# Rows of 320 columns instead of 384: the last transposition takes columns 192 to 320, and the low parts go to the lower half of the partitions

## Chip, core and metric

The kernel runs on one core of a Trainium2 chip. The metric is the device time of one execution in microseconds (us), as the median of several runs. TensorE is called PE, VectorE DVE, ScalarE ACT, GpSimd POOL and SyncE SP, as in the profile.

## The reference

Three stages run one after the other: a gated linear attention over 768 steps for 2 x 8 heads of 40 columns, a mixture of 8 experts of which each of the 1536 rows takes two, and a feed-forward layer with the activation h·cos(h). A row has 320 columns throughout.

```python
for t in range(S):                       # attention, S = 768
    m_new = np.maximum(f_gate[:, :, t] + m, i_gate[:, :, t])
    ...
    h_tilde = np.einsum('bhde,bhe->bhd', C, qt)
    denom = np.maximum(np.abs(nq), 1.0)
    y[:, :, t] = o * h_tilde / denom

for e in range(E):                       # experts, E = 8, 320 -> 1024 -> 320
    for k in range(2):
        mask = top2[:, k] == e
        h = np.maximum(x[mask] @ w1[e], 0.0)
        out[mask] += top2_w[mask, k, None] * (h @ w2[e])

h = x @ w_in                             # 320 -> 2048 -> 320
g = h * np.cos(h)
return (g @ w_out).astype(np.float32)
```

## The kernel before

**Split numbers.** The matrix products must come out in float32 precision. Each operand is split into a high part, rounded to the format that PE multiplies fast, and a low part, the rest. `mm1` (L585) forms a product of rows and first weights out of eight matmuls: high times high, high times low and low times high for two blocks of 128 columns, and two for the last block.

**The last block.** 320 columns are two blocks of 128 and one of 64. In the last one the partitions 0 to 63 hold the high parts of columns 256 to 319 and the partitions 64 to 127 the low parts of the same columns; the weights lie there twice (`pack`, L1118). One matmul over 128 partitions then gives high times weight plus low times weight. For this, every row is 384 columns long (`KW`) before the change: its last 64 columns are a copy of columns 256 to 319, and transposing columns 256 to 383 puts the same numbers in both halves. `prep_x` (L547) transposes three blocks of up to 128 rows into PSUM, ACT copies them rounded into `xh` (L553), DVE writes the low parts of the first two blocks (L554) and the low parts of partitions 64 to 127 of the third in place (L555).

**Where rows are made.** In the attention a chunk n of 128 rows ends in `mk_y` (L315): DVE writes 320 columns of the tile `xt` (L327), POOL copies the last 64 (L329), SP stores the rows in `XD` in DRAM (L330). PE transposes the same tile for the router (`rt_a`, L337). The experts' rows are fetched from `XD` by indirect DMAs that POOL issues (`gather`, L537). After the experts `comb` (L669) adds the two results of a row on DVE (L674), a second DVE instruction copies the last 64 columns (L675), and `comb_t` hands the tile to `prep_x`.

**Order.** Each engine works through its own queue in order. The order is written out by hand: `att_step` (L850) for the twelve chunks, and a table of steps (`put`, L905) for the rest. In POOL's queue the copy of chunk n stands between the state decay of the next chunk (L277) and two triangular masks (`mk_w`, L210); behind these come a weight split (`split`, L573, L582) and, in chunk 9, the first two gathers. In SP's queue the store of chunk n (L330) stands ahead of weight loads (L528). In the last phase `comb` runs beside the conversion of the last layer's weights (`conv_ops`, L697) and the layer's own steps (`moe2_step`, L787).

Of the kernel before, what the change touches and what calls it, by code (L numbers as in the profile page):

```python
# [9 lines left out]
FT = mybir.dt.float32  # L10
# [10 lines left out]
C = 128  # L21
# [19 lines left out]
def tile_mlstm_moe_moe2(ctx, tc, qk, kv, og, gi, gf, wcat, noise, wm1, wm2, cst, out):  # L41
# [105 lines left out]
    XD = dr.tile([B * S, KW], FT, name="xd")  # L147
# [167 lines left out]
    def mk_y(n):  # L315
# [10 lines left out]
        x = d["x"] = mp.tile([128, KW], FT, name="xt", bufs=3)  # L326
        V.scalar_tensor_tensor(out=x[:, :DM].rearrange("p (h e) -> p h e", e=D), in0=pv[:, :, 0:D], scalar=0.5,  # L327
                               in1=o, op0=OP.mult, op1=OP.mult)
        G.tensor_copy(x[:, DM:KW], x[:, 256:DM])  # L329
# [6 lines left out]

    def rt_a(n, ps_=None):  # L337
        b, c = divmod(n, NC)
        d = L[n]
        p = (ps_ or psM)()  # L340
        for k in range(3):
            T.transpose(p[:, 128 * k:128 * k + 128], d["x"][:, 128 * k:128 * k + 128], ident)
        d["xT"] = ap_.tile([128, 3, 128], FT, name="xTt", bufs=2)
        A.activation(d["xT"], p[:, :KW].rearrange("p (k t) -> p k t", t=128), AF.Copy)
# [192 lines left out]
    def gather(g, i):  # L537
# [3 lines left out]
        t = mp.tile([128, KW], FT, name="xgt", tag="xg", bufs=6)  # L541
# [5 lines left out]
    def prep_x(src, np_, xh, xl, n0, ps_=None):  # L547
        p = (ps_ or psM)()
        pv = p[:, :3 * np_].rearrange("p (k t) -> p k t", t=np_)
        for k in range(3):  # L550
            T.transpose(pv[:, k, :], src[:np_, 128 * k:128 * k + 128], ident[:np_, :np_])  # L551
# [3 lines left out]
        V.tensor_tensor(out=xh[64:128, 2, sl], in0=pv[64:128, 2, :], in1=xh[64:128, 2, sl].bitcast(FT),  # L555
# [53 lines left out]
    def fin1(g):  # L609
        d = GX[g]  # L610
        for i, n in enumerate(groups[g][1]):
            t = (mp.tile([128, KW], FT, name="xt", bufs=3) if i == 3 else
# [56 lines left out]
    def comb(b, c):  # L669
# [3 lines left out]
        x = mp.tile([128, KW], FT, name="xt", bufs=3)  # L673
        V.scalar_tensor_tensor(out=x[:, :DM], in0=y1, scalar=r["w"][:, 1, c:c + 1], in1=y0, op0=OP.mult, op1=OP.add)  # L674
        V.tensor_copy(x[:, DM:KW], x[:, 256:DM])  # L675
# [354 lines left out]
    with tc.If(over > 0):  # L1030
# [9 lines left out]
        for b in range(B):  # L1040
            with tc.For_i(0, NC, 1) as it:
                x = mp.tile([128, KW], FT, name="xt", bufs=3)
# [4 lines left out]
                for k in range(3):  # L1047
                    T.transpose(p[:, 128 * k:128 * k + 128], x[:, 128 * k:128 * k + 128], ident)
                xT = wp.tile([128, 384], FT, name="m_t", tag="ct", bufs=3)
                A.activation(xT, p[:, :KW], AF.Copy)  # L1050
                x2 = mp.tile([128, KW], FT, name="xt", bufs=3)
                V.memset(x2, 0.0)
                for e in range(E):
                    acc = psA()
                    for f in range(8):
# [3 lines left out]
                        for k in range(3):  # L1059
                            n = 64 if k == 2 else 128  # L1060
                            T.matmul(p[:, :C], w[:n, 128 * k:128 * k + 128], xT[:n, 128 * k:128 * k + 128],
# [6 lines left out]
                V.tensor_copy(x2[:, DM:KW], x2[:, 256:DM])  # L1068
# [21 lines left out]
def layout(inp):  # L1090
# [23 lines left out]
    w[0] = wg[0:128]; w[1] = wg[128:256]; w[2, :64] = wg[256:]  # L1114
# [44 lines left out]
```

## Time and profile before

| | |
|---|---|
| median of 3 runs | 524.96 us (522.64 to 525.19) |
| the profiled execution | 525.03 us, of which the trace spans 523.3 us |
| PE busy | 490.2 us (94% of the span) |
| DVE busy | 372.1 us (71%) |
| ACT busy | 325.7 us (62%) |
| POOL busy | 278.5 us (53%) |
| chain that ended last | PE 69%, DVE 14%, DMA 7% |

The attention ends at about 110 us, the experts run from 94 to 334 us and the last layer from 334 to 516 us, with overlaps. A time at the start of a row counts from the start of the span. A gap ahead of an instruction stands in brackets behind it, with what ended it.

### The profile page before, as it was taken

The page shows a single profiled execution, that of the slowest core. Times are in us where ns is not written, and L with a number is a line of the kernel's source. Part 1 is how long each engine was busy: PE and PEld are TensorE (multiplying, and loading weights), DVE is VectorE, ACT ScalarE, POOL GpSimd, SP SyncE. Part 2 cuts the span into 40 slices and gives each one's busy share as a digit, 9 for nine tenths or more (in the row PEclk, how much of TensorE's full clock was granted, in tenths as well). Part 3 has the DMA queues.
Part 4 walks back from the last instruction along what each step waited for, and adds up shares of the span by engine and source line. Part 5 has one row for each costly group of instructions (what it writes and reads, how often), then busy time and mean ns, then how long its engine had stood idle before and what let it go on. Part 6 is the DMA issues. An engine that isn't in the chain of part 4 may idle for free.

```text
span 523.3 us, 9036 instructions
## 1 busy us (share of the span) xinstructions
PE 490.2 (94%) x3198; PEld 468.1 (89%) x3198; DVE 372.1 (71%) x791; ACT 325.7 (62%) x695; POOL 278.5 (53%) x246
## 2 busy tenths in 40 slices
PE   4799998999999999999999987999999999999994
PEld 3688887999899999999999976899999999999994
DVE  8774497678378777777775689688856665787772
ACT  3647867466465454545454655578787777777772
POOL 6445468665846867685857696274365347300000
PEclk9999999899999999999999999999999999999998
DMA  6789894695563828291929193030021003001001
GB/s 182 209 281 266 279 278 155 188 363 172 216 248 117 313 88 330 69 372 44 380 88 319 42 360 105 29 115 14 0 76 39 1 8 95 13 2 39 1 1 44
DMA packets 25909, 77.69 MB, mean 148 GB/s; under 512 B 3872, under 2 KB 11552, under 8 KB 25856
## 3 DMA queue, kind: packets, MB, share of 16 engines
q1 hardware_dynamic: 22752, 67.50, 37.2%
q0 software_dynamic: 3104, 9.54, 6.1%
q8 instruction: 27, 0.44, 0.3%
q14 instruction: 26, 0.21, 0.1%
HBM read 67.41 MB, written 9.62 MB: 147 GB/s over the span
## 4 chain that ended last, share of the span: by engine, by line
PE 69%; DVE 14%; DMA 7%; issue 4%; ACT 3%; POOL 2%; SPq 0%; DVEq 0%; POOLq 0%; ACTq 0%
PE pS L589 31%; PE pA L598 9%; PE pA L595 9%; PE pA L594 9%; DMA gb<-gd 2%; DMA xgt<-xd,idx 2%; PE pM L551 2%; PE pS L310 2%; PE pA L247 1%; PE pM L351 1%; PE pA L607 1%; PE pA L606 1%; POOL wl L582 1%; DVE xt L674 1%; DVE c_t L713 1%
## 5 line engine op out<-in xcount | busy, mean ns | idle before, releaser
L582 POOL TENSOR_TENSOR wl<-wraw,wh 128x704 fp32r<-128x704 f32 x69 | 122.9, 1787 | 59.9 <-ACT wh L580 56.3
L644 DVE SCALAR_TENSOR_TENSOR hb<-pS,hb 128x384 fp32r<-128x384 f32 (+2 forms) x128 | 45.9, 390 | 46.4 <-ACT hb L641 45.8
L580 ACT ACTIVATE wh<-wraw 128x704 fp32r<-128x704 f32 x80 | 62.8, 785 | 14.6 <-PE pA L606 8.2
L589 PE MATMUL pS<-xh,wh 128*128 128x448 f32 (+1 forms) x240 | 69.5, 344 | 0.4 <-ACT xh L553 0.4
L589 PE MATMUL pS<-xh,wl 128*128 128x448 f32 (+1 forms) x240 | 66.3, 330 | 0.9 <-POOL wl L582 0.9
L589 PE MATMUL pS<-xh,w 128*128 128x384 f32 x288 | 66.4, 339 | 0.5 <-DVE m_t L754 0.5
L594 PE MATMUL pA<-wh,hb 128*128 128x320 f32 x208 | 62.2, 309 | 0.0
L595 PE MATMUL pA<-wl,hb 128*128 128x320 f32 x208 | 62.2, 309 | 0.0
L739 ACT ACTIVATE m_t<-pS,magic 128x384 f32<-128x384 f32 x64 | 37.1, 579 | 30.4 <-PE pS L589 29.3
L641 ACT ACTIVATE hb<-pS 128x448 fp32r<-128x448 f32 (+1 forms) x80 | 37.6, 471 | 26.9 <-PE pS L589 20.0
L589 PEld LDWEIGHTS pS<-xh,w 128*128 128x128 f32 x288 | 50.0, 188 | 1.2 <-DVE m_t L754 1.1
L598 PE MATMUL pA<-wh,hb 128*128 128x320 f32 x208 | 44.3, 313 | 4.0 <-DVE hb L644 4.0
L754 DVE SCALAR_TENSOR_TENSOR m_t<-m_t,pS 128x384 f32<-128x384 f32 x64 | 35.4, 553 | 15.4 <-ACT m_t L753 15.1
L589 PEld LDWEIGHTS pS<-xh,wl 128*128 128x128 f32 x240 | 43.1, 190 | 3.3 <-POOL wl L582 1.1
L740 DVE TENSOR_SCALAR m_t<-m_t 128x384 f32<-128x384 f32 x64 | 23.3, 365 | 28.8 <-ACT m_t L739 28.6
L589 PEld LDWEIGHTS pS<-xh,wh 128*128 128x128 f32 x240 | 40.9, 190 | 1.4 <-ACT xh L553 0.6
L760 POOL TENSOR_TENSOR wl<-m_t,wh 128x384 fp32r<-128x384 f32 x25 | 25.4, 1017 | 31.0 <-ACT wh L758 21.7
L589 PE MATMUL pS<-xl,wh 128*128 128x448 f32 (+1 forms) x160 | 39.6, 329 | 0.0
L594 PEld LDWEIGHTS pA<-wh,hb 128*128 128x128 f32 x208 | 38.6, 186 | 0.6
L595 PEld LDWEIGHTS pA<-wl,hb 128*128 128x128 f32 x208 | 38.7, 186 | 0.6
L598 PEld LDWEIGHTS pA<-wh,hb 128*128 128x128 f32 x208 | 33.0, 186 | 6.0 <-DVE hb L644 5.9
L542 POOL DMA_INDIRECT xgt<-xd,idx x28 | 34.0, 1215 | 7.8 <-issue 3.4
(203 smaller groups left out, 1251.0 us busy)
## 6 DMA issues: line engine op xcount, KB each, us to landing
wraw<-wm SPq DMA_DIRECT2D x36, 704.0 KB
raw<-wm SPq DMA_DIRECT2D x16, 704.0 KB
qk<-qk SPq DMA_DIRECT2D x24, 240.0 KB
gb<-gd SPq DMA_DIRECT2D x10, 512.0 KB
kv<-kv SPq DMA_DIRECT2D x12, 324.0 KB
yd<-yt SPq DMA_DIRECT2D x22, 160.0 KB
wraw<-wm SPq DMA_DIRECT2D x8, 352.0 KB
xd<-xt SPq DMA_DIRECT2D x12, 192.0 KB
```

Of the source, the lines that this page charges most:

```text
L542: G.indirect_dma_start(out=t[:n, :], out_offset=None, in_=XD[0:S, :] if g < 2 else XD[:, :], in_offset=bass.IndirectOffsetOnAxis(ap=(idxe ...
L580: A.activation(wh, raw[:, f, :], AF.Copy)
L582: eng.tensor_tensor(out=wl, in0=raw[:, f, :], in1=wh.bitcast(FT), op=OP.subtract)
L589: T.matmul(p[:, :n], w[:, 128 * k:128 * k + 128], x[:, m, :], start=(i == 0), stop=(i == 7))
L594: T.matmul(a[:n, :DM], hh[:, s], wh[:, KW:], start=first, stop=False)
L595: T.matmul(a[:n, :DM], hh[:, s], wl[:, KW:], start=False, stop=False)
L598: T.matmul(a[:n, :DM], hl[:, s], wh[:, KW:], start=False, stop=last)
L641: A.activation(hh[:, :n], p[:, :n], AF.Relu)
L644: V.scalar_tensor_tensor(out=hb[:, o:o + z - a], in0=p[:, a:z], scalar=0.0, in1=hh[:, a:z].bitcast(FT), op0=OP.max, op1=OP.subtract)
L739: A.activation(t, m["p"], AF.Identity, bias=magic, scale=0.5 / PI)
L754: V.scalar_tensor_tensor(out=s, in0=s, scalar=1.0, in1=m["p"], op0=OP.subtract, op1=OP.mult)
L760: eng.tensor_tensor(out=m["hl"], in0=m["t"], in1=m["hh"].bitcast(FT), op=OP.subtract)
```

## The change

The rows of `xt`, `xg` and `XD` become 320 columns long. The two copies are gone. The third transposition takes columns 192 to 319: its partitions 64 to 127 get columns 256 to 319, and its partitions 0 to 63 get columns 192 to 255, which the second block has already. ACT copies all three blocks as before. DVE then writes the low parts, which it works out from partitions 64 to 127, to partitions 0 to 63. In the router the last block's weights move to partitions 64 to 127 and the others are zero. A path that runs only when an expert gets too many rows is changed alike and does not run here.

```diff
-    XD = dr.tile([B * S, KW], FT, name="xd")
+    XD = dr.tile([B * S, DM], FT, name="xd")
...
-        x = d["x"] = mp.tile([128, KW], FT, name="xt", bufs=3)
-        V.scalar_tensor_tensor(out=x[:, :DM].rearrange("p (h e) -> p h e", e=D), in0=pv[:, :, 0:D], scalar=0.5,
+        x = d["x"] = mp.tile([128, DM], FT, name="xt", bufs=3)
+        V.scalar_tensor_tensor(out=x.rearrange("p (h e) -> p h e", e=D), in0=pv[:, :, 0:D], scalar=0.5,
                                in1=o, op0=OP.mult, op1=OP.mult)
-        G.tensor_copy(x[:, DM:KW], x[:, 256:DM])
         Y.dma_start(XD[b * S + c * C:b * S + (c + 1) * C, :], x)
...
+    def cols(x, n, k):
+
+        c0 = min(128 * k, DM - 128)
+        return x[:n, c0:c0 + 128]
...
-            T.transpose(p[:, 128 * k:128 * k + 128], d["x"][:, 128 * k:128 * k + 128], ident)
+            T.transpose(p[:, 128 * k:128 * k + 128], cols(d["x"], 128, k), ident)
...
-        t = mp.tile([128, KW], FT, name="xgt", tag="xg", bufs=6)
+        t = mp.tile([128, DM], FT, name="xgt", tag="xg", bufs=6)
...
-            T.transpose(pv[:, k, :], src[:np_, 128 * k:128 * k + 128], ident[:np_, :np_])
+            T.transpose(pv[:, k, :], cols(src, np_, k), ident[:np_, :np_])
         sl = slice(n0, n0 + np_)
         A.activation(xh[:, :, sl], pv, AF.Copy)
         V.tensor_tensor(out=xl[:, :, sl], in0=pv[:, 0:2, :], in1=xh[:, 0:2, sl].bitcast(FT), op=OP.subtract)
-        V.tensor_tensor(out=xh[64:128, 2, sl], in0=pv[64:128, 2, :], in1=xh[64:128, 2, sl].bitcast(FT),
+
+        V.tensor_tensor(out=xh[0:64, 2, sl], in0=pv[64:128, 2, :], in1=xh[64:128, 2, sl].bitcast(FT),
                         op=OP.subtract)
...
-        x = mp.tile([128, KW], FT, name="xt", bufs=3)
-        V.scalar_tensor_tensor(out=x[:, :DM], in0=y1, scalar=r["w"][:, 1, c:c + 1], in1=y0, op0=OP.mult, op1=OP.add)
-        V.tensor_copy(x[:, DM:KW], x[:, 256:DM])
+        x = mp.tile([128, DM], FT, name="xt", bufs=3)
+        V.scalar_tensor_tensor(out=x, in0=y1, scalar=r["w"][:, 1, c:c + 1], in1=y0, op0=OP.mult, op1=OP.add)
...
-    w[0] = wg[0:128]; w[1] = wg[128:256]; w[2, :64] = wg[256:]
+    w[0] = wg[0:128]; w[1] = wg[128:256]; w[2, 64:] = wg[256:]
```

What moves is seen on three queues. POOL's queue at chunks 8 and 9, where the masks (L210) are followed by the first weight split (L582, after the change L587) and the first gathers (L542, after it L546):

```order
-L329 COPY xt<-xt 128x64 [waits DMAHW0_49,DVE_49,Pool_49]
-L210 AFFINE_SELECT wt<-wt 128x512 [waits Activation_49] x2
-L582 TENSOR_TENSOR wl<-wraw,wh 128x704 [waits DMAHW6_49,Activation_49]
+L210 AFFINE_SELECT wt<-wt 128x512 [waits Activation_49,Pool_49]
+L210 AFFINE_SELECT wt<-wt 128x512 [waits Activation_49]
+L587 TENSOR_TENSOR wl<-wraw,wh 128x704 [waits DMAHW6_49,Activation_49]
 L229 TENSOR_TENSOR kb_95<-kv,kdec 128x8x40 [waits DMAHW2_49]
 L277 TENSOR_TENSOR st_99<-st_101,get 40x4x41 [waits DVE_49,PE_49,Activation_49]
 L277 TENSOR_TENSOR st_99<-st_101,get 40x4x41 [waits DVE_49,Activation_49,Pool_49]
-L542 DMA xgt<-xd,idxe 128x384 [waits DVE_49,Pool_49]
-L542 DMA xgt<-xd,idxe 112x384
-L329 COPY xt<-xt 128x64 [waits DMAHW5_49,DVE_49]
+L546 DMA xgt<-xd,idxe 128x320 [waits DMAHW0_49,DMAHW3_49,DVE_49,Pool_49]
+L546 DMA xgt<-xd,idxe 112x320
```

The masks no longer stand behind an instruction that waits for DVE; the first gather now names the stores of its rows itself, which the copies had waited for on its behalf.

SP's queue at chunk 9, the store of the rows and three weight loads behind it, first before and then after:

```order
L330 DMA xd<-xt 128x384 [waits DMAHW2_49,Pool_49]
L528 DMA wraw<-wm 128x704 [waits DMAHW3_49]
L528 DMA wraw<-wm 128x704 [waits DMAHW4_49]
L528 DMA wraw<-wm 128x704 [waits DMAHW5_49]
```

```order
L329 DMA xd<-xt 128x320 [waits DMAHW2_49,DVE_49]
L532 DMA wraw<-wm 128x704 [waits DMAHW3_49]
L532 DMA wraw<-wm 128x704 [waits DMAHW4_49]
L532 DMA wraw<-wm 128x704 [waits DMAHW5_49]
```

The store waits for DVE instead of POOL; the order is the same.

DVE's queue at the first two results of `comb` (L674, after the change L679), with a step of the weight conversion behind each (`w2q` and `c_t`), first before and then after:

```order
L674 SCALAR_TENSOR_TENSOR xt<-yg,r_w_1075 128x320 [waits DMASW1_49,Activation_49]
L675 COPY xt<-xt 128x64 [waits DVE_49]
L723 TENSOR_TENSOR w2q<-c_t_3676,w2q 128x704 [waits DMAHW3_49,DMAHW2_49,Activation_49]
L644 SCALAR_TENSOR_TENSOR hb<-pS,hb 128x240 [waits Activation_49]
L619 COPY yt<-pA 112x320 [waits DMAHW1_49,PE_49]
L674 SCALAR_TENSOR_TENSOR xt<-yg,r_w_1075 128x320 [waits DMAHW2_49,DMASW3_49,Activation_49]
L675 COPY xt<-xt 128x64 [waits DVE_49]
L713 SCALAR_TENSOR_TENSOR c_t_3725<-raw_3583,c_t_3725 128x704
```

```order
L679 SCALAR_TENSOR_TENSOR xt<-yg,r_w_1065 128x320 [waits DMASW1_49,Activation_49]
L727 TENSOR_TENSOR w2q<-c_t_3664,w2q 128x704 [waits DMAHW3_49,DMAHW2_49,Activation_49]
L649 SCALAR_TENSOR_TENSOR hb<-pS,hb 128x240 [waits Activation_49]
L624 COPY yt<-pA 112x320 [waits DMAHW1_49,PE_49]
L679 SCALAR_TENSOR_TENSOR xt<-yg,r_w_1065 128x320 [waits DMAHW2_49,DMASW3_49,Activation_49]
L717 SCALAR_TENSOR_TENSOR c_t_3713<-raw_3571,c_t_3713 128x704 [waits DVE_49]
```

The copies drop out, and the instruction behind the second one carries the wait for DVE that the copy had carried. PE's and ACT's queues keep their instructions and their order.

## Rows read from the trace of the kernel before

**Rows 1.** Busy time by stretch: stretch, length, engines, TensorE clock, DMA share, GB/s

```profile
75.00:92.00 17.00, 14.16 (x120) 12.44 (x118) 13.05 (x28) 10.96 (x31) 14.39 (x19) 1.00 0.60 192
92.00:96.00 4.00, 3.65 (x19) 3.65 (x20) 2.90 (x8) 1.69 (x4) 3.00 (x3) 0.57 0.89 266
133.00:300.00 167.00, 166.52 (x1006) 159.69 (x1005) 118.83 (x204) 87.69 (x154) 116.67 (x72) 1.00 0.55 204
300.00:340.00 40.00, 33.77 (x243) 31.47 (x241) 32.48 (x51) 22.22 (x45) 24.20 (x17) 1.00 0.46 166
355.00:375.00 20.00, 19.16 (x121) 18.57 (x120) 18.04 (x35) 15.95 (x34) 6.35 (x7) 1.00 0.01 4
375.00:515.00 140.00, 139.86 (x874) 138.26 (x873) 95.23 (x203) 106.93 (x222) 41.05 (x41) 1.00 0.09 26
```

**Rows 2.** Groups by line and shape: busy us, mean ns, idle before it

```profile
L555 DVE TENSOR_TENSOR xh<-pM,xh 64x128 fp32r<-64x128 f32 x30 | 8.8, 295 | 0.4
...
L675 DVE COPY xt<-xt 128x64 f32<-128x64 f32 x12 | 3.7, 312 | 0.4
L329 POOL COPY xt<-xt 128x64 f32<-128x64 f32 x12 | 3.7, 307 | 26.0 <-DVE xt L327 17.7 <-issue 8.3
```

**Rows 3.** POOL's timeline, chunks 8 and 9: start, us, instruction, gap before

```profile
81.44 0.84 POOL L329 COPY xt<-xt 128x64 f32<-128x64 f32 x1 [1.50 <-issue]
...
87.80 1.23 POOL L542 DMA_INDIRECT xgt<-xd,idxe  x1 [0.61 <-DVE den L323]
...
90.32 0.23 POOL L329 COPY xt<-xt 128x64 f32<-128x64 f32 x1
```

**Rows 4.** PE's timeline: the waits for POOL and for gathers

```profile
85.83 0.96 PE L266 MATMUL pS<-kv,kb 128*104 128x82 f32 x8 [1.05 <-POOL kb L229]
...
92.35 0.82 PE L551 MATMUL pA<-ident,xgt 112*128 112x112 f32 x3 [0.62 <-DMA xgt<-xd,idxe]
...
176.44 0.52 PE L551 MATMUL pM<-ident,xgt 128*128 128x128 f32 x3 [0.48 <-DMA xgt<-xd,idx]
```

**Rows 5.** DVE's timeline, chunk 9: the gather's indices and the rows' end

```profile
86.68 0.17 DVE L511 TENSOR_SCALAR idxe<-idx 128x4 uint32<-128x4 f32 x1
...
88.01 0.49 DVE L327 SCALAR_TENSOR_TENSOR xt<-pS,ogt 128x320 f32<-128x320 f32 x1
```

**Rows 6.** SP's timeline, chunk 9: the three weight loads behind the store

```profile
90.96 1.46 SPq L528 DMA_DIRECT2D wraw<-wm  x3
```

**Rows 7.** Landing of the gathers issued at 89.33 and at 100.42, us

```profile
DMA to landing us min/median/max: 3.0/3.0/3.0
...
DMA to landing us min/median/max: 5.6/5.6/5.6
```

**Rows 8.** DVE's timeline, last phase: copies and what stands around them

```profile
317.38 1.59 DVE L675 COPY xt<-xt 128x64 f32<-128x64 f32 x1
...
321.70 0.20 DVE L675 COPY xt<-xt 128x64 f32<-128x64 f32 x1
...
328.93 1.93 DVE L723 TENSOR_TENSOR w2q<-c_t,w2q 128x704 fp32r<-128x704 f32 x1
...
369.01 0.42 DVE L554 TENSOR_TENSOR xl<-pM,xh 128x256 fp32r<-128x256 f32 x1 [0.15 <-ACT xh L553]
```

**Rows 9.** POOL's timeline, the weight splits beside the first copy and beside L723

```profile
317.02 1.89 POOL L582 TENSOR_TENSOR wl<-wraw,wh 128x704 fp32r<-128x704 f32 x1
...
328.39 1.72 POOL L582 TENSOR_TENSOR wl<-wraw,wh 128x704 fp32r<-128x704 f32 x1 [3.92 <-ACT wh L580]
```

**Rows 10.** PE's timeline, last phase: its waits for DVE

```profile
325.54 0.56 PE L598 MATMUL pA<-wh,hb 128*128 128x320 f32 x2 [0.44 <-DVE hb L644]
...
372.00 0.96 PE L589 MATMUL pS<-xh,w2q 128*128 128x384 f32 x4 [0.83 <-DVE m_t L754]
```

**Rows 11.** DVE's timeline, start: same shape, without and with another partition block

```profile
9.73 0.28 DVE L109 TENSOR_TENSOR g_all<-g_all 16x128 f32<-16x128 f32 x1
10.04 0.28 DVE L110 TENSOR_TENSOR g_all<-g_all 16x128 f32<-16x128 f32 x1
```

More of the change, by code (lines that the diff above doesn't have):

```diff
@@ L611, in fin1 @@
         for i, n in enumerate(groups[g][1]):
-            t = (mp.tile([128, KW], FT, name="xt", bufs=3) if i == 3 else
+            t = (mp.tile([128, DM], FT, name="xt", bufs=3) if i == 3 else
                  mp.tile([128, DM], FT, name="yt", tag="yt", bufs=3))
@@ L1041, in tile_mlstm_moe_moe2 @@
             with tc.For_i(0, NC, 1) as it:
-                x = mp.tile([128, KW], FT, name="xt", bufs=3)
+                x = mp.tile([128, DM], FT, name="xt", bufs=3)
                 Y.dma_start(x, XD[bass.ds(it * C + b * S, C), :])
@@ L1047, in tile_mlstm_moe_moe2 @@
                 for k in range(3):
-                    T.transpose(p[:, 128 * k:128 * k + 128], x[:, 128 * k:128 * k + 128], ident)
+                    T.transpose(p[:, 128 * k:128 * k + 128], cols(x, 128, k), ident)
                 xT = wp.tile([128, 384], FT, name="m_t", tag="ct", bufs=3)
                 A.activation(xT, p[:, :KW], AF.Copy)
-                x2 = mp.tile([128, KW], FT, name="xt", bufs=3)
+                x2 = mp.tile([128, DM], FT, name="xt", bufs=3)
                 V.memset(x2, 0.0)
@@ L1059, in tile_mlstm_moe_moe2 @@
                         for k in range(3):
-                            n = 64 if k == 2 else 128
-                            T.matmul(p[:, :C], w[:n, 128 * k:128 * k + 128], xT[:n, 128 * k:128 * k + 128],
+                            r = slice(64 * (k == 2), 128)
+                            T.matmul(p[:, :C], w[r, 128 * k:128 * k + 128], xT[r, 128 * k:128 * k + 128],
                                      start=(k == 0), stop=(k == 2))
@@ L1067, in tile_mlstm_moe_moe2 @@
                                            in1=x2[:, :DM], op0=OP.mult, op1=OP.add)
-                V.tensor_copy(x2[:, DM:KW], x2[:, 256:DM])
                 d = {}
```

## Prediction

> **What bounds the kernel now.** I read the page's shares first, then the busy time by stretch, then the waits and timelines of the stretches in which PE idles. PE is full for 166.52 of the 167 us of the experts' main part and for 139.86 of the 140 us after 375 us [rows 1]. In these stretches a saving on another engine, or in a DMA that already comes in time, is worth nothing, and no matmul or transposition is removed. The change can gain only where PE idles and something that it removes or moves ends the wait: 75 to 92 us (17.00 less 14.16 is 2.84 us idle), 300 to 340 us (6.23 us idle, DVE busy 32.48 of 40) and 355 to 375 us (0.84 us idle, DVE busy 18.04 of 20) [rows 1]. Together that is some 10 us, of which most belongs to waits that the copies do not cause. One gather of the main part adds a wait of 0.48 us [rows 4].
>
> **What is removed, as busy time.** Twelve copies on POOL, 3.7 us, and twelve on DVE, 3.7 us [rows 2]. Each row of XD loses 256 bytes: 12 stores of 32 KB less and 32 gathers of up to 32 KB less. That is not yet time; each place is taken by itself.
>
> **The copies on POOL.** They stand in POOL's queue behind a wait for DVE: 17.7 of the 26.0 us of idle time ahead of them was ended by L327 [rows 2]. Up to 75 us I cost this at nothing: PE is busy with the attention's matmuls there and none of its waits was for the copy. At chunk 8 POOL is late. It idles 1.50 us, then the copy takes 0.84 us, 81.44 to 82.28 [rows 3], and the masks, the first weight split and `kb` come behind it; PE waits 1.05 us for `kb` at 85.83 [rows 4]. Without the copy the masks start earlier. But PE then only reaches its next wait sooner: the second transposition of gathered rows, at 92.35, waits for its gather [rows 4], and that chain sets the time. The first gather was issued at 87.80 [rows 3], while its indices were ready at 86.68 + 0.17 = 86.85 [rows 5]. So an earlier POOL can pull the gathers forward by at most 87.80 - 86.85 = 0.95 us. The least is nothing, if what held POOL until 87.80 was DVE, as the wait's label says. I take 0.4 us, about the middle.
>
> **The stores.** At chunk 9 the store of the rows waited for the copy that POOL ran behind both gathers, until 90.32 + 0.23 = 90.55 [rows 3]; now it waits for DVE, which ended at 88.01 + 0.49 = 88.50 [rows 5]. Queued behind it on SP are three weight loads, issued from 90.96 [rows 6]. They leave 2.05 us earlier, and so can meet the gathers. I cost that at nothing in the forecast, since a transfer issued at 88.9 would move most of its data after the gathers, as the heavy traffic of 92 to 96 us (266 GB/s) followed the loads of 90.96 [rows 1, 6]; the other case is a rival. At the other chunks an earlier store gains nothing, as PE waits for no load there.
>
> **Shorter rows.** The one wait of the main part for a gather is 0.48 us at 176.44 [rows 4]. A row that is a sixth shorter takes something off it, between 0 and the whole 0.48; I take 0.2 us, because other loads share that transfer. The other gathers of that stretch land in time.
>
> **The copies on DVE.** Of the twelve, the six after 375 us lie beside a full PE [rows 1]: nothing. Three stand between 317 and 325 us. The first lasts 1.59 us against 0.20 us for the second [rows 8], and that looks like the prize. It started at 317.38, while POOL ran a weight split from 317.02 to 318.91 [rows 9], and it ended at 318.97, just behind it. So it was held. What comes next without it is L723, and an L723 at 328.93, beside another split of POOL that ended at 330.11, lasted 1.93 us and ended 0.75 us behind it [rows 8, 9]. So L723 will be held by the same split, and the gain is only what the copy did after the split, some 0.06 us. I take 0.1 us. The Trainium skill says the same more generally (SBUF — State Buffer, "SBUF: two separate sides"): GpSimd and VectorE instructions in a two-port mode or with two SBUF inputs take a shared port pair as an exclusive lock, and the loser waits for the whole instruction. It speaks against this change, and the trace agrees (1.59 us against 0.20). Read without the lock, the first copy would give 1.59 us instead of 0.1.
>
> The second and third copy are free of that: 0.20 us each [rows 8]. PE waits for DVE 0.44 us at 325.54 [rows 10]; of the 0.4 us I take half to reach it, since the additions between them are also held by splits. So this stretch gives 0.1 + 0.2 = 0.3 us, with bounds 0 and 0.5.
>
> The last three copies stand between 355 and 375 us, where DVE is 90% busy. Two of them are followed by a DVE instruction that waits for ACT (0.15 us at 369.01 [rows 8]), that is, for a transposition by a PE that was not late: the gain is spent in that wait. The third is followed by no such wait, and PE waits 0.83 us for DVE at 372.00 [rows 10]: 0.2 us, with bounds 0 and 0.6 (all three).
>
> **The moved low parts.** L555 now reads partitions 64 to 127 and writes 0 to 63. It lasts 295 ns [rows 2] and runs 44 times. The nearest row of DVE that writes another block of partitions than it reads is L110 (0 to 15, to 32 to 47): 0.28 us, as its neighbour L109 of the same shape without a shift [rows 11]. So I cost it at nothing. L555 is no busier, no longer and waits for the same ACT copy. The transpositions read other columns of the same tile at the same size: nothing.
>
> **The sum.** 0.4 + 0.2 + 0.3 + 0.2 = 1.1 us off the profiled execution's own 525.03 us gives 523.9. That execution lies 0.07 us above the median of 524.96, so I leave it there. From the bounds alone the gain is between 0 and 0.95 + 0.48 + 0.5 + 0.6 = 2.5 us: 522.5 to 525.0.
>
> **Rivals.**
>
> *The clock's dip goes.* Between 92 and 96 us the granted clock is 0.57, between the levels of 1.2 and 2.4 GHz, after PE had idled 2.84 of 17 us [rows 1]. The dip costs 4.00 x (1 - 0.57) = 1.7 us. If `kb` comes in time and the gathers earlier, PE idles less ahead of it and the dip may shrink or go. For it speaks that 1.05 of the 2.84 us was the wait for `kb` [rows 4]; against it, that this wait is likely to reappear as a longer one for the gather. Time: 523.9 - 1.7 = 522.2.
>
> *The weight loads meet the gathers (slower).* Place: chunk 9. The three loads now leave at about 88.9, beside gathers issued between 87.4 and 89. A gather at 89.33 without such company landed after 3.0 us, one at 100.42 behind other transfers after 5.6 us [rows 7]. If the second gather takes the latter, PE's wait at 92.35 grows by 5.6 - 3.0 = 2.6 us: 523.9 + 2.6 = 526.5. It decides from the point at which the loads' data begin to flow before the second gather's are through. For it speaks that SP is free then; against it, the delay between issue and heavy traffic seen above. By the Trainium skill (DMA: Bandwidth & Descriptors, "Queues, rings and completion order") a DMA engine takes turns between its queues packet by packet, which would make this cheaper; the landing of 5.6 us says that company costs, whatever the turns.
>
> *Nothing arrives.* The earlier POOL only meets DVE's short instructions elsewhere and holds them, the gather stays bound to DVE, and the 0.2 us pieces sink in other waits. Time: 525.0.
>
> **Chances.** Forecast 0.55, dip gone 0.17, loads meet gathers 0.14, nothing arrives 0.10, something that I have not seen 0.04. A measurement of this kernel can tell 0.5%, that is 2.6 us, from no change: faster means below 522.3, slower above 527.6. Faster takes most of the dip's 0.17 and the edge of the forecast: 0.21. Slower takes the far end of the collision and half of the unseen: 0.06. The rest, 0.73, is no change that can be told. The range reaches from just below the dip's time, 522.0, to just below the collision's, 526.3.
>
> **What would show it.** Right: POOL's masks at chunk 8 start before 81 us and PE's wait at 85.83 shrinks; the first gather is issued within 0.6 us of its indices; L723 beside POOL's split near 317 us lasts over 1.5 us in the copy's place; L555 stays at 295 ns; PE stays full from 133 to 300 and after 375 us. Wrong: L555 takes longer; the gathers of chunk 9 land after more than 4 us; the clock stays full between 92 and 96 us; or the stretch from 300 to 340 us loses more than 0.5 us, which would mean that the lock is not what held the first copy.

## The result, and the profile after

| | before | after | ratio, 95% interval |
|---|---|---|---|
| first comparison, median of 5 and 5 runs | 524.37 us | 528.19 us | 1.0083 [1.0057, 1.0109] |
| a second comparison, of 24 and 7 runs | 523.58 us | 526.69 us | 1.0059 [1.0036, 1.0082] |
| the profiled execution of after | | 526.06 us, span 524.0 us | |

The change makes the kernel some 3 to 4 us slower. Of that, some 0.4 us lie outside the span of the traces: the time is longer than the span by 1.65 to 1.83 us in every run of the kernel before that has its span on record, and by 2.06 to 2.24 us in every run of after. No run says what these 0.4 us are. The forecast was 523.9 us, with a range of 522.0 to 526.3. The trace shown here is that of the fastest of the first five executions; a second trace of the same kernel, with a span of 525.9 us, is told of below.

The busy time by stretch, after; it answers to [rows 1] and has its columns:

```profile
75.00:92.00 17.00, 14.71 (x105) 13.27 (x105) 12.00 (x27) 10.24 (x29) 11.32 (x13) 0.84 0.53 177
92.00:96.00 4.00, 1.74 (x9) 1.45 (x8) 0.82 (x3) 0.94 (x2) 1.55 (x2) 0.50 0.34 136
133.00:300.00 167.00, 166.53 (x1007) 159.43 (x1006) 120.65 (x208) 87.93 (x154) 116.94 (x73) 1.00 0.54 199
300.00:340.00 40.00, 36.58 (x257) 34.99 (x257) 31.95 (x49) 23.34 (x46) 27.52 (x18) 0.96 0.47 168
355.00:375.00 20.00, 19.44 (x122) 19.02 (x122) 17.19 (x33) 16.59 (x34) 7.64 (x8) 1.00 0.03 9
375.00:515.00 140.00, 140.00 (x878) 138.93 (x877) 95.36 (x199) 107.83 (x224) 41.16 (x41) 1.00 0.09 26
```

Between 92 and 96 us PE is busy for 1.74 us of 4 where it was for 3.65, and the clock is at its lower level, 1.2 GHz (0.50). From 300 us on PE idles less than before. So the loss lies in one place, around 90 us. PE's timeline there, after, against [rows 4]:

```profile
83.73 0.93 PE L266 MATMUL pS<-kv,kb 128*104 128x82 f32 x8 [0.35 <-issue]
85.70 0.42 PE L306 MATMUL pS<-st,qtt 128*128 128x82 f32 x2 [1.03 <-DVE r_hi L513]
91.39 0.90 PE L555 MATMUL pA<-ident,xgt 128*128 128x128 f32 x3 [0.49 <-DMA xgt<-xd,idxe]
94.56 0.82 PE L555 MATMUL pA<-ident,xgt 112*128 112x112 f32 x3 [2.26 <-DMA xgt<-xd,idxe]
```

`kb` no longer makes PE wait 1.05 us, and its matmuls start 2.1 us earlier than before (83.73 against 85.83). Most of these 2.1 us arose before: at chunk 8 the like matmuls already start 1.9 us earlier (75.79 against 77.70), and in a second trace of after they start at 77.54. But the second block of gathered rows is transposed 2.2 us later (94.56 against 92.35). In the trace of after, POOL's timeline (first weight split and the two gathers), SP's (the three weight loads) and DVE's (the second half of the router's mask `r_am`, and the gather's indices); they answer to [rows 3], [rows 6] and [rows 5]:

```profile
79.74 1.68 POOL L587 TENSOR_TENSOR wl<-wraw,wh 128x704 fp32r<-128x704 f32 x1
...
87.01 1.15 POOL L546 DMA_INDIRECT xgt<-xd,idxe  x1 [2.56 <-issue]
88.46 0.94 POOL L546 DMA_INDIRECT xgt<-xd,idxe  x1 [0.30 <-issue]
...
87.86 1.41 SPq L532 DMA_DIRECT2D wraw<-wm  x3
...
79.77 2.46 DVE L483 TENSOR_TENSOR r_am<-r_pp,cc 128x768 bf16<-128x768 f32 x1
...
85.91 0.17 DVE L515 TENSOR_SCALAR idxe<-idx 128x4 uint32<-128x4 f32 x1
```

Two things are new. The loads are issued from 87.86, between the two gathers, where they had been issued behind them. And the mask takes 2.46 us beside POOL's split, which ends at 81.42. Before the change it took 0.95 us, as this line of DVE's timeline of before has it:

```profile
81.23 0.95 DVE L479 TENSOR_TENSOR r_am<-r_pp,cc 128x768 bf16<-128x768 f32 x1
```

**Four intervals.** Executions of one kernel differ by some 2 us, and part of that arises before chunk 8: its matmuls with `kb` start at 75.79 and at 77.54 us in two traces of one kernel, after. So I compare intervals between fixed points of one trace, all starts from the timelines of PE and DVE: I from the matmuls with `kb` at chunk 8 (77.70 in before) to the gather's indices (86.68); II from there to the transposition of the second gathered block (92.35); III from there to the router's matmuls of chunk 10 (102.33); IV from there to one of the last transpositions of `comb`'s rows (465.10).

| kernel | I | II | III | I to III | IV |
|---|---|---|---|---|---|
| before | 8.98 | 5.67 | 9.98 | 24.63 | 362.77 |
| before, second trace | 8.98 | 5.64 | 9.27 | 23.89 | 362.18 |
| before, loads ahead | 8.99 | 5.59 | 9.28 | 23.86 | 362.98 |
| before, copy on DVE | 10.49 | 8.82 | 10.56 | 29.87 | 362.81 |
| before, last phase as after | 8.98 | 5.92 | 10.07 | 24.97 | 360.60 |
| after, POOL copy put back | 8.97 | 5.56 | 10.07 | 24.60 | 360.48 |
| after | 10.12 | 8.65 | 11.14 | 29.91 | 359.97 |
| after, second trace | 10.11 | 8.45 | 11.04 | 29.60 | 360.50 |
| after, split moved | 8.90 | 8.92 | 10.54 | 28.36 | 361.01 |
| after, one load left | 10.12 | 6.61 | 10.87 | 27.60 | 360.54 |
| after, loads behind the gathers | 10.11 | - | - | 25.89 | 361.71 |
| after, loads ahead | 10.11 | 5.76 | 11.13 | 27.00 | 361.54 |
| after, loads ahead and split moved | 8.91 | 5.62 | 9.89 | 24.42 | 360.77 |
| the same, second trace | 8.90 | 5.82 | 10.09 | 24.81 | 361.03 |

(Where II and III are missing, both blocks are transposed in one row of the timeline.) Means of two traces of after less those of the first three rows: I +1.1 (the indices come later), II +2.9 (the gather lands later), III +1.6 (longer at the lower clock), together +5.6. IV is shorter, by 2.4 in these and by 1.9 in the mean of all ten traces without the copies (360.8) against the four with them (362.7). So about +3.2 to +3.7 us remain. The two comparisons measured +3.8 and +3.1, which is 3.4 and 2.7 without the 0.4 us outside the span.

### The profile page after: what moved, and what is told of

It reads as the page before. It is cut to its first block, busy times and chain, and to the rows that moved or that the text cites. A ratio compares the mean times of both kernels' runs of the same rounds, so it can differ in the third digit from the quotient of the medians.

```text
span 524.0 us, 9010 instructions
## 1 busy us (share of the span) xinstructions
PE 493.4 (94%) x3198; PEld 472.7 (90%) x3198; DVE 372.6 (71%) x779; ACT 326.1 (62%) x695; POOL 277.2 (53%) x234
## 4 chain that ended last, share of the span: by engine, by line
PE 74%; DVE 12%; DMA 4%; ACT 4%; issue 3%; POOL 1%; SPq 0%; DVEq 0%; POOLq 0%; ACTq 0%
PE pS L594 34%; PE pA L603 10%; PE pA L599 10%; PE pA L600 10%; PE pM L555 2%; PE pS L310 1%; PE pA L612 1%; PE pA L611 1%; ACT wt L209 1%; DMA xgt<-xd,idxe 1%; PE pM L355 1%; DMA gb<-gd 1%; DVE r_am L483 1%; DMA yg<-yd,r_pos 1%; DVE ppt L256 1%
## 5 line engine op out<-in xcount | busy, mean ns | idle before, releaser
L587 POOL TENSOR_TENSOR wl<-wraw,wh 128x704 fp32r<-128x704 f32 x69 | 124.0, 1804 | 64.6 <-ACT wh L585 57.9
L599 PEld LDWEIGHTS pA<-wh,hb 128*128 128x128 f32 x208 | 39.1, 188 | 0.6
L546 POOL DMA_INDIRECT xgt<-xd,idx x28 | 34.1, 1217 | 7.8 <-DVE idx L519 3.2
L745 DVE SCALAR_TENSOR_TENSOR m_t<-pS,m_t 128x384 f32<-128x384 f32 x64 | 35.7, 558 | 2.2
```

Source lines behind the costliest of these rows:

```text
L546: G.indirect_dma_start(out=t[:n, :], out_offset=None, in_=XD[0:S, :] if g < 2 else XD[:, :], in_offset=bass.IndirectOffsetOnAxis(ap=(idxe ...
L587: eng.tensor_tensor(out=wl, in0=raw[:, f, :], in1=wh.bitcast(FT), op=OP.subtract)
L599: T.matmul(a[:n, :DM], hh[:, s], wh[:, KW:], start=first, stop=False)
L745: V.scalar_tensor_tensor(out=t, in0=m["p"], scalar=0.5 / PI, in1=t, op0=OP.mult, op1=OP.subtract)
```

## The experiments

My theory after the result: the store that no longer waits for POOL lets the three weight loads leave beside the first two gathers. The rivals: rows of 320 columns are slower to store and to gather, the moved low parts cost something, or the loss is elsewhere.

**The loads moved ahead.** The first expert's eight loads keep their order, but the last three stand behind the stores of chunks 7 and 8.

```diff
-        put((6, 7, 8, 8, 8, 9, 9, 9)[i], load_w, 0, i, 1)
+        put((6, 7, 7, 7, 8, 8, 8, 8)[i], load_w, 0, i, 1)
```

> The kernel after with one edit: of the first expert's eight weight loads (one f block each) the three that stand behind chunk 9's store now stand behind the stores of chunks 7 and 8 (steps 6,7,7,7,8,8,8,8 instead of 6,7,8,8,8,9,9,9). Nothing heavy leaves SP between the first two gathers and their use. Theory 'loads meet the gathers': in the profile of after the second gathered block is transposed at 94.56 us behind a wait of 2.26 us, before the change at 92.35 behind 0.62, and the longer low-clock stretch behind it costs another 1.2; with the loads away the second gather lands about 3 us after its issue, the transposition comes at 91.5 to 92.5, and the time falls by 3 to 5 us, to 523 to 525 us. Rival 'shorter rows are slower to store and gather' (1280 bytes a row instead of 1536): the loads do not matter, the second gather still takes some 6 us, the time stays at 527 to 529. Rival 'something after 110 us, the low parts written to other partitions for one': the wait at chunk 9 goes but at most 2 us of time come back, 526 or more.

Measured: 524.47 us against 523.9, ratio 1.0004 [0.9985, 1.0022]. PE's timeline of this kernel:

```profile
83.90 0.93 PE L266 MATMUL pS<-kv,kb 128*104 128x82 f32 x8 [0.35 <-issue]
...
90.55 0.77 PE L555 MATMUL pA<-ident,xgt 128*128 128x128 f32 x3 [1.48 <-DMA xgt<-xd,idxe]
91.84 0.82 PE L555 MATMUL pA<-ident,xgt 112*128 112x112 f32 x3 [0.52 <-DMA xgt<-xd,idxe]
```

II falls from 8.65 to 5.76, the value of before, with rows of 320 columns: neither these nor the store itself, which still leaves at 87.6, delay the gather. The loads do. But I and III stay long, so something else costs too.

**The loads moved behind the gathers.**

```diff
-        put((6, 7, 8, 8, 8, 9, 9, 9)[i], load_w, 0, i, 1)
+        put((6, 7, 8, 8, 8, 10, 10, 10)[i], load_w, 0, i, 1)
```

> The kernel after with the same three weight loads moved the other way, behind the store of chunk 10 (steps 6,7,8,8,8,10,10,10), some 9 us later and behind the first two gathers. Theory 'loads meet the gathers': the first two gathers land in about 3 us, the transposition of the second comes at 91.5 to 92.5 us; but the loads now leave beside the gathers of the second expert, issued near 100 us, which already took 5.6 us before the change, and whose rows are needed only near 120 us: nothing lost there. 523 to 526 us. Rival 'shorter rows': 527 to 529, the second gather still landing after some 6 us. A loss at about 105 to 115 us, where the first expert's last blocks are needed, would speak for neither, but for loads that come too late.

Measured: 525.79 us against 523.9, ratio 1.0032 [1.0011, 1.0054]. PE's timeline at the gathered rows, and the stretch of 24 to 34 us:

```profile
95.44 1.41 PE L555 MATMUL pA<-ident,xgt 128*128 128x128 f32 x6
...
24.00:34.00 10.00, 9.25 (x45) 8.47 (x45) 4.44 (x9) 1.62 (x4) 2.51 (x4) 0.66 0.79 279
```

Both blocks are transposed in one go without a wait, which fits the theory. In this execution the clock was low early (0.66 from 24 to 34 us; in after it was 1.00 there), and the matmuls with `kb` at chunk 8 start at 79.96 us, against 75.79 in after. The median is 1.3 us above that of the run before. Some 0.7 us of it the trace shows: the moved loads come late for the first expert's last blocks, so ACT waits for them, as it does neither in after nor with the loads ahead, and from the router's matmuls of chunk 10 to those of chunk 11 it is 6.19 us where it is 5.48 in after:

```profile
109.55 0.79 ACT L585 ACTIVATE wh<-wraw 128x704 fp32r<-128x704 f32 x1 [2.58 <-DMA wraw<-wm]
```

**The POOL copy put back, with short rows.** POOL copies columns 256 to 319 onto themselves, and the store waits for it as before the change.

```diff
+        G.tensor_copy(x[:, 256:DM], x[:, 256:DM])
         Y.dma_start(XD[b * S + c * C:b * S + (c + 1) * C, :], x)
```

> The kernel after with a POOL copy put back in front of the store (columns 256 to 319 onto themselves, so the row stays 320 long): store, weight loads and the router's transposition wait for POOL as before the change, while rows, DVE copies and low parts stay as after. Theory 'the earlier store': the second gather lands in about 3 us again, the low-clock stretch is back to some 4 us, and the time is that of before less the small gains of the removed DVE copies and shorter rows: 522.5 to 525 us. Rival 'shorter rows' or 'moved low parts': the time stays at 527 to 529, since both are still in.

Measured: 522.66 us against 523.9, ratio 0.9983 [0.9968, 0.9997]. The second gathered block, PE:

```profile
92.65 0.51 PE L556 MATMUL pA<-ident,xgt 112*128 112x112 f32 x3 [0.66 <-DMA xgt<-xd,idxe]
```

I to III are those of before, and IV is short. So the whole loss came with taking the copy off POOL, and the rest of the change gains about 1 us by the time (0.2 to 1.7 by the interval) and 1.6 us by the span (520.7 against 522.3, means of the runs).

**The copy of before on DVE.** The other way round: the kernel before, with its long rows, and only POOL freed.

```diff
-        G.tensor_copy(x[:, DM:KW], x[:, 256:DM])
+        V.tensor_copy(x[:, DM:KW], x[:, 256:DM])
```

> The kernel before with one edit: the copy of a row's last 64 columns in the attention runs on DVE, right behind the instruction that writes the row, instead of on POOL. Rows stay 384 columns, low parts and the last phase's copies stay as before. The store and the weight loads behind it leave at chunk 9 some 1.8 us earlier, and POOL is free of the wait for DVE, nearly as after. Theory 'the earlier store': most of the loss appears without any shorter row, 526 to 529 us, with a second gather that lands after more than 5 us. Rival 'shorter rows' or 'moved low parts': no loss, 523 to 525.5.

Measured: 530.14 us against 523.9, ratio 1.0121 [1.0098, 1.0144]. PE's waits, and SP's loads:

```profile
93.31 0.60 PE L551 MATMUL pA<-ident,xgt 128*128 128x128 f32 x3 [3.12 <-DMA xgt<-xd,idxe]
96.02 0.82 PE L551 MATMUL pA<-ident,xgt 112*128 112x112 f32 x3 [2.11 <-DMA xgt<-xd,idxe]
...
89.37 1.40 SPq L528 DMA_DIRECT2D wraw<-wm  x3
```

More than the whole loss appears without any of the change's other features, and more than the 526 to 529 expected. I to III is 29.87, as after; IV is that of before.

**One load left behind the store of chunk 9.**

```diff
-        put((6, 7, 8, 8, 8, 9, 9, 9)[i], load_w, 0, i, 1)
+        put((6, 7, 7, 8, 8, 8, 8, 9)[i], load_w, 0, i, 1)
```

> The kernel after with one of the three weight loads left behind chunk 9's store and two moved ahead (steps 6,7,7,8,8,8,8,9). A dose between none (524.5 us, the second gathered block transposed 7.9 us behind kb's first matmuls of chunk 9) and three (526.7 to 528.2, 10.6 to 10.8 us). Theory 'the loads share the DMA engines with the gathers, and each of their 0.36 MB is time': the second gathered block at 8.5 to 9.3 us behind kb's, 525 to 526 us. Rival 'any company is enough, the size does not matter': as with three, over 10 us, 526.5 or more. Rival 'one load still gets through ahead of the gathers': as with none, 8.1 or less, 524.5.

Measured: 525.9 us against 524.6, ratio 1.0023 [1.0002, 1.0044]. The landing of its two gathers, us:

```profile
DMA to landing us min/median/max: 4.1/4.1/4.1
...
DMA to landing us min/median/max: 4.0/4.0/4.0
```

II is 6.61, between the 5.6 to 5.9 without a load and the 8.5 to 8.9 with three; the size counts. The second block stands 8.79 us behind `kb`'s matmuls of chunk 9, inside the theory's 8.5 to 9.3.

**The first weight split moved behind the gathers**, the loads left as after. In after POOL's split and DVE's mask start within 0.03 us of each other; here they do not meet.

```diff
-    put(8, split, 0)
+    put(9, split, 0)
```

> The kernel after with the first weight split moved behind the gathers, and the three loads left where the change has them. It takes the part that lets DVE's mask run (1.50 us instead of 2.46) apart from the part that keeps the loads away. Theory 'the two add up': gathers, store and loads all come 1 us earlier together, the collision stays, a wait of over 2 us for the second gather remains, and the time falls by 1 to 2.5 us below after's 526.7 to 528.2: 525 to 526.5. Rival 'the collision sets the end alone': no gain, 526.5 to 528. Rival 'the split beside the mask was the loss': 523.5 or less.

Measured: 526.88 us against 524.6, ratio 1.0036 [1.0016, 1.0056]. The mask on DVE, the second gathered block on PE, and the landing of the second gather:

```profile
81.54 1.50 DVE L483 TENSOR_TENSOR r_am<-r_pp,cc 128x768 bf16<-128x768 f32 x1
...
95.39 0.82 PE L555 MATMUL pA<-ident,xgt 112*128 112x112 f32 x3 [2.79 <-DMA xgt<-xd,idxe]
...
DMA to landing us min/median/max: 6.3/6.3/6.3
```

I falls from 10.12 to 8.90, so the split beside the mask held back the indices. II stays at 8.92, since gathers and loads move together. By the ratios (1.0036 against 1.0059 and 1.0083) there may be a gain over after of 1 to 2.5 us; the intervals overlap with the nearer one, and 526.88 lies just above the theory's 525 to 526.5, where the rival without a gain begins. So the time does not decide between them; that the split cost something is shown by I.

**Both together**, loads ahead and split moved, on two chips.

```diff
-        put((6, 7, 8, 8, 8, 9, 9, 9)[i], load_w, 0, i, 1)
+        put((6, 7, 7, 7, 8, 8, 8, 8)[i], load_w, 0, i, 1)
...
-    put(8, split, 0)
+    put(9, split, 0)
```

> The kernel after with the three weight loads moved ahead (as in the run that moved them behind the stores of chunks 7 and 8: 524.5 us) and with the first weight split (ACT's copy and POOL's subtraction, L585 and L587) moved from step 8 to step 9, behind the two gathers. In the profile of after POOL ran that split from 79.74 to 81.42 us, and DVE's mask r_am beside it took 2.46 us instead of 0.95. Theory 'a split holds the mask, and the gathers follow the indices by a fixed 0.93 us': r_am takes about 1 us, the indices come 1.5 us earlier, the gathers too, the second gathered block is transposed about 1.3 to 1.5 us earlier and the time falls to 522.5 to 523.5 us. Rival 'something else on POOL or ACT binds the indices, or another DVE instruction is held instead': the indices move by less than 0.5 us, 524 to 525 us. Rival 'the splits come too late for the first expert': PE waits for wl near 92 us, 525 us or more.

> The kernel after with the three loads moved ahead and the first split behind the gathers, unchanged, on another chip: 522.22 us against 523.58 the first time, ratio 0.9977 with an interval of 0.9957 to 0.9997 that hardly leaves out no change. Theory 'faster than both': the ratio lies between 0.995 and 0.999 again. Rival 'an accident of the executions': 0.999 or more.

Measured: 522.22 us against 523.58, ratio 0.9977 [0.9957, 0.9997], and 524.49 against 524.6, ratio 0.9986 [0.9961, 1.0011]. POOL's `kb`, DVE's mask and PE's second block in the first of these traces:

```profile
80.08 0.72 POOL L229 TENSOR_TENSOR kb<-kv,kdec 128x320 f32<-128x320 f32 x1
...
80.11 1.50 DVE L483 TENSOR_TENSOR r_am<-r_pp,cc 128x768 bf16<-128x768 f32 x1
...
90.66 0.82 PE L555 MATMUL pA<-ident,xgt 112*128 112x112 f32 x3 [0.62 <-DMA xgt<-xd,idxe]
```

I to III is 24.4 and 24.8, back to before's level, and IV stays short. It is faster than after. That it beats before is likely, by the intervals of the traces, but only one of the two ratios shows it. The mask still takes 1.50 us, now beside `kb`: it ends at 81.61, 0.81 us behind `kb`'s end at 80.80, just as in after it ended (82.23) 0.81 us behind the split's end (81.42). So it waits for POOL's instruction and then runs; the 1 us that was expected did not come, because another instruction of POOL stood in the split's place.

**The loads moved ahead in the kernel before**, as a control.

```diff
-        put((6, 7, 8, 8, 8, 9, 9, 9)[i], load_w, 0, i, 1)
+        put((6, 7, 7, 7, 8, 8, 8, 8)[i], load_w, 0, i, 1)
```

> The kernel before with nothing but the three weight loads of step 9 moved behind the stores of chunks 7 and 8. A control for the runs that moved them in the kernel after. In before the loads leave at 90.96 us, behind the gathers, so they delay no gather that PE waits for. Theory 'the loads cost only what they do to the first two gathers': no change, 523 to 524.5 us, the second gathered block transposed within 0.3 us of where it stood against kb's matmuls (6.5 us behind them). Rival 'moving the loads is a gain of its own, through the traffic of 92 to 96 us': 522.5 or less.

Measured: 524.91 us against 524.6, ratio 0.9995 [0.9975, 1.0014]; II is 5.59. Moving the loads gains nothing by itself.

**The last phase alone.** The kernel before with the new columns of the transposition, the moved low parts and without DVE's copies; rows stay 384 long and POOL's copies stay. Against the kernel after:

```diff
-    XD = dr.tile([B * S, DM], FT, name="xd")
+    XD = dr.tile([B * S, KW], FT, name="xd")
...
+        G.tensor_copy(x[:, DM:KW], x[:, 256:DM])
         Y.dma_start(XD[b * S + c * C:b * S + (c + 1) * C, :], x)
...
-        t = mp.tile([128, DM], FT, name="xgt", tag="xg", bufs=6)
+        t = mp.tile([128, KW], FT, name="xgt", tag="xg", bufs=6)
```

> The kernel before with the last phase's part of the change alone: the transposition takes columns 192 to 319, the low parts go to partitions 0 to 63, and the twelve DVE copies behind comb are gone; rows stay 384 columns in memory, POOL's copies and with them the stores stay as before. Against the run with the POOL copy put back (522.7 us) it differs in the length of the rows alone. Theory: moved low parts cost nothing and the DVE copies give 0.3 us near 310, 0.3 near 370 and 0.6 between 375 and 465: 522.9 to 524 us, about 1.2 below before; the wait of 0.48 us for a gather at 176 us stays, since rows are long. Rival 'the shorter rows gave it': as before, 523.9 to 524.5, with L555's successor over 0.3 us if the moved low parts cost something.

Measured: 522.93 us against 523.58, ratio 0.9996 [0.9977, 1.0015]. The ratio decides nothing here, in part because the time again holds 0.4 us more outside the span; by the span it is 1.0 us below before (521.0 against 522.0, means of the runs). IV is 360.60, against 360.48 with short rows, and two traces of after alone differ by more (359.97 and 360.50). So no gain from the length of the rows shows in IV. What shortens IV is in this kernel too, and of its parts the moved low parts take as long as before (below), which leaves DVE's copies for most of it; 0.5 us of it are open (*Shorter rows*, below). One expectation failed: the wait for a gather at 176 us was to stay, since the rows are long, and it is gone:

```profile
175.24 0.49 PE L556 MATMUL pM<-ident,xgt 128*128 128x128 f32 x3
```

PE between two steps of the last layer, first in before (DVE's copy at 461.43 is one of the six after 375 us), then here:

```profile
461.64 0.60 PE L598 MATMUL pA<-w,wl 128*128 128x320 f32 x3
462.26 0.97 PE L589 MATMUL pS<-xh,w2q 128*128 128x384 f32 x4
```

```profile
459.24 0.60 PE L604 MATMUL pA<-w,wl 128*128 128x320 f32 x3
459.70 0.96 PE L595 MATMUL pS<-xh,w2q 128*128 128x384 f32 x4
```

From the three matmuls to the next step it is 0.62 us with the copy and 0.46 without it. The rows print no wait in either, and the stretch counted as full. Five of the six copies lie between the two transpositions below, and behind four of them the step comes 0.13 to 0.19 us later in the kernels with the copies. It adds up, in before and here:

```profile
407.80 0.49 PE L551 MATMUL pM<-ident,xt 128*128 128x128 f32 x3
...
465.10 0.49 PE L551 MATMUL pM<-ident,xt 128*128 128x128 f32 x3
```

```profile
405.88 0.49 PE L556 MATMUL pM<-ident,xt 128*128 128x128 f32 x3
...
462.52 0.49 PE L556 MATMUL pM<-ident,xt 128*128 128x128 f32 x3
```

57.30 us before, 56.64 here: 0.66 us.

**Second traces of both kernels, unchanged.**

> The kernel before, unchanged, for a second trace. It tells which differences between the two traces stand for the change and which for the execution: PE's wait of 2.02 us for a load at 24.76 and of 0.91 us at 44.40, which the other kernels' traces do not show, and the low-clock stretch at 92 to 96 us. Theory 'a matter of the execution': at least one of the two waits is gone or smaller by half, without any change of the kernel. Rival 'the change shortens them': both stand as they were, 2.0 and 0.9 us.

> The kernel after, unchanged, for a second trace and more runs. The first trace belongs to its fastest execution (526.06 us of a median of 528.19), and two other traces show a low-clock stretch near 15 to 30 us that costs up to 4 us and is not in it. Theory 'the early store explains all': waits for the two gathers between 90 and 96 us of 2.5 to 5 us and a low-clock stretch around them in this trace too, and a median of 527 to 529. Rival 'most of the loss is a low clock in the first 40 us, which the change makes more frequent': the low stretch stands there in this trace, and the start of chunk 1 lags that of before by over 2 us.

Before, second trace: one run of 523.41 us. PE's two early waits and the stretch of 92 to 96 us:

```profile
23.38 0.67 PE L247 MATMUL pA<-qk 128*128 128x256 f32 x2 [0.62 <-DMA qk<-qk]
...
43.42 0.94 PE L351 MATMUL pM<-wc,xTt 128*128 128x128 f32 x6 [1.39 <-ACT xTt L344]
...
92.00:96.00 4.00, 3.77 (x29) 3.41 (x29) 3.50 (x10) 2.92 (x7) 3.91 (x3) 1.00 0.85 271
```

The wait for the load was 2.02 us in the first trace and is 0.62 now; the next was 0.91 and is 1.39. And the low clock at 92 to 96 us is gone (1.00 against 0.57 in [rows 1]), in the same kernel with the same waits at chunk 9. So both are matters of the execution. After, second trace, PE at the second block, and the stretch around it:

```profile
96.10 0.82 PE L555 MATMUL pA<-ident,xgt 112*128 112x112 f32 x3 [2.27 <-DMA xgt<-xd,idxe]
...
86.00:102.00 16.00, 12.70 (x64) 11.85 (x63) 7.94 (x24) 7.78 (x20) 8.85 (x9) 0.57 0.32 110
```

The wait stands again (2.27 against 2.26), and the clock is low for most of 16 us. From 24 to 34 us it was full. The rival of a low clock early, made more frequent by the change, has nothing for it in the two traces; the other executions of after have no trace. It is not ruled out either: of the 14 traces, five have a stretch at the lower level before 35 us, one of them a trace of the kernel before with the loads ahead (0.83 from 24 to 34 us), four of them traces of kernels made from after.

## Why the prediction failed, by its steps

**The stores: the step that failed.** It saw that the store and the three loads would leave 2 us earlier, and costed that at nothing, on the ground that their data would move after the gathers, since the heavy traffic of 92 to 96 us followed loads issued from 90.96 [rows 1, 6]. That ground fails by its own rows. Between this issue and the heavy traffic lie 92.00 - 90.96 = 1.0 us, and 92 was only where I had cut the stretch. Loads issued at 88.9 would then move from 89.9 on, and a gather issued by 89 that lands after 3.0 us is under way until 92. What the DMA engines moved between 86 and 95 us in slices of 0.225 us, in GB/s, first after and then with the loads ahead:

```profile
GB/s 0 0 0 0 0 0 0 0 0 0 216 347 165 114 182 108 116 214 259 288 361 338 326 413 413 400 401 401 426 400 457 395 167 30 0 0 0 0 0 0
```

```profile
GB/s 150 25 0 0 0 0 0 0 0 0 6 319 341 63 205 137 296 91 0 264 199 177 34 0 0 0 0 0 0 0 0 0 0 0 0 0 0 0 0 0
```

In after the traffic grows from 88.3 us on, 0.8 us behind the store's issue at 87.47, and ends near 93.5; with the loads ahead it ends near 91. PE goes on 1.1 and 0.7 us behind that end. So the gather is done only about when the loads are. The queues show it directly: q0 is that of the gathers, q1 that of the loads and the store. In after the second gather was issued at 88.46, 0.6 us behind the first load. Packets that begin, their MB and their share of 16 engines, from 91 to 92.75 us and from there to 94:

```profile
q1 hardware_dynamic: 284, 0.71, 102.3%
...
q0 software_dynamic: 48, 0.14, 29.0%
q1 hardware_dynamic: 46, 0.08, 17.7%
```

For 1.75 us only loads moved, and the 0.14 MB of the second gather, 112 rows of 1280 bytes, came behind them. With the loads ahead these packets moved from 90.3 to 91.5. The rival *the weight loads meet the gathers* had place, mechanism and sign right, and +2.6 us for the landing against +2.9 measured (II). I gave it 0.14, because what I held against it was the same reading. Its time, 526.5, lay below what came, because it held neither the later indices nor the longer time at the lower clock.

Beside it I cited the Trainium skill (DMA: Bandwidth & Descriptors, "Queues, rings and completion order"): engines take turns between queues packet by packet, which would make company cheap for a small transfer. The runs do not bear that out: a gather landed after 2.9 to 3.3 us without loads beside it, after 4.0 and 4.1 beside one load, and the second of two after 5.9 and 6.3 beside three. In the 1.75 us above it got no turn in after; with the copy on DVE in the kernel before both queues moved packets in each half microsecond from 91.5 to 95.5, and the block came as late (II 8.82). What decides between the two no run shows.

**The copies on POOL: right in part, wrong in sign.** The masks started at 77.68 us and `kb`'s wait shrank, as said. But the indices came 1.1 us later (I), not the gathers 0.4 us earlier. Two readings failed. First, the 0.95 us from the indices to the first gather was not POOL's lateness: in after it is 87.01 - (85.91 + 0.17) = 0.93, though POOL had been idle for 2.56 us. It is 0.92 to 0.95 in all 14 traces, so the 0 to 0.95 that I allowed was never to be had. Second, a POOL that is earlier meets other instructions of DVE. Its split started 0.03 us ahead of the mask and held it for 1.5 us. The hint stood in [rows 3]: the copy at 81.44 took 0.84 us and a like one 0.23, because the mask, started at 81.23, was then ahead of it. My rival *nothing arrives* named the mechanism and priced it at zero. Here the Trainium skill (SBUF — State Buffer, "SBUF: two separate sides") says what the runs show: whichever of the two starts first gets the shared ports for its whole instruction. I had applied that rule to the last phase, and not to the place where the change moved POOL.

The prediction also left out that PE waited for the copy itself, 0.92 us at chunk 9 in before:

```profile
90.60 0.33 PE L342 MATMUL pM<-ident,xt 128*128 128x128 f32 x1 [0.92 <-POOL xt L329]
```

That wait is gone in after, and gains nothing: PE comes to the gathered blocks sooner and waits there.

**The clock.** The dip after 92 us was priced at 1.7 us if it went. It grew, to 1.6 us more of III. But in before it is there in one trace and not in the other, so it was no property of the kernel to begin with. The price was too high as well: III is 9.98 us with the dip and 9.27 without, 0.7 us less.

**Shorter rows.** 0.2 us forecast: not shown. In the four traces with DVE's copies, all with long rows, the wait of 0.48 us at 176 us is 0.24 to 0.59, and the block comes 4.2 us behind the one ahead of it on average, against 3.7 in the ten others. But the last phase alone, with long rows, has no wait there, and with the loads ahead in after the block comes 4.05 us behind, with short ones. So some 0.5 us of IV lie there, and their cause is open.

**The copies on DVE, 300 to 375 us: right.** By the lock the first copy's 1.59 us were to move to L723, now L727, with a gain of 0.06 us. DVE and POOL after, against [rows 8, 9]:

```profile
319.70 2.38 DVE L727 TENSOR_TENSOR w2q<-c_t,w2q 128x704 fp32r<-128x704 f32 x1
...
319.46 1.87 POOL L587 TENSOR_TENSOR wl<-wraw,wh 128x704 fp32r<-128x704 f32 x1
```

L727 lasts 2.38 us, where copy and L723 had taken 1.59 + 0.88. From the gathered block that stands at 306.66 us in before to `comb`'s third transposition (329.83) it is 22.5 to 22.8 us in the ten traces without the copies and 23.1 to 23.5 in the four with them: 0.5 on average, against the 0.3 forecast. From 360 to 375 us the gain is 0.1 to 0.4, forecast 0.2; PE's wait of 0.83 us [rows 10] is 0.56 to 0.60 in all traces without the copies.

**The copies on DVE after 375 us: wrong.** Costed at nothing, since PE was full; they gave 0.66 us. With the 0.5 at 176 us, the 0.5 at 306 to 330 and the 0.1 to 0.4 at 360 to 375 this makes up the 1.9 of IV.

**The moved low parts: right.** L560 lasts 293 ns, against 295 for L555 [rows 2].

**The sum.** Forecast for I to III -0.4, measured +5.6. Forecast for the rest -0.7, measured -1.9 to -2.4. With the POOL copy put back, the kernel ran at 522.66, 1.2 us below before.

## What to carry to other kernels

When an edit frees a queue, list what stands behind the freed wait in every queue and ask what of it will now run beside the critical transfer: a wait that looks useless may be what keeps large loads behind a small urgent gather. When an engine that shares ports gets earlier, look up which instructions it will run beside at the new time, on the chain that sets the end. And read a gain of under 1 us from intervals between fixed points of one trace; the medians of this kernel cannot tell it.

## What the runs showed of the hardware

- A gather of 112 to 128 rows landed after 2.9 to 3.3 us without loads beside it, and after 4.0 to 4.1 beside one load of 0.36 MB. Beside three the second of two landed after 5.9 and 6.3. POOL issues the gathers and SP the loads, on different queues.
- In after, 0.71 MB of loads moved in 1.75 us in which no packet of a gather moved, though POOL had issued one 2.5 us before.
- From the end of the instruction that writes the indices to the start of the gather's issue passed 0.92 to 0.95 us in 14 traces, whether POOL had been idle for 0.61 or for 2.56 us.
- A stretch in which PE counts as busy throughout can still hold waits: in a row of three matmuls that take 0.60 us, the next instruction can start 0.46 us behind their start, so up to 0.16 us of waiting is not shown as idle. Five copies of 0.20 us cost 0.66 us there.
- The clock fell to its lower level in some executions of a kernel and not in others: at 92 to 96 us 0.57 and 1.00 in two traces of before, with PE busy for 14.16 and 13.84 of the 17 us ahead. Five of 14 traces have a lower stretch before 35 us. In the one where it is longest (0.66 from 24 to 34 us), the `kb` matmuls of chunk 8 start at 79.96 us, against 75.79 to 77.70 in the nine traces that have none.
